# A softcap attention with a spectral mix on one core: the scores and values of the last 64 keys, and the fourth score burst, in other places of TensorE's order

## The chip, the cores and the metric

The kernel runs on one core of a Trainium2 chip. The metric is the device time of one execution in microseconds; the time given for a kernel is the median of its runs.

## The reference

For each of 8 batches and 12 heads, with 448 positions and a head size of 64, the attention is

```python
scores = cap * tanh((q @ k.T / 8) / cap)
attn = exp(scores - max) / sum
x = attn @ v
```

The heads are put side by side (x is 448 x 768 for a batch), and then comes a mix:

```python
theta = x @ w_theta
y = w_tok_r @ (x * cos(theta)) + w_tok_i @ (x * sin(theta))
u = x + y
out = u + relu(u @ w_ch)
```

Everything is float32.

## The kernel before

**Steps.** The attention is done in 24 steps, one for four heads (two pairs, i = 0 and 1; a pair is two heads h on the two halves of the partitions). Three steps make a batch. The mix of a batch runs four steps and more behind its attention, and its products fill TensorE while ScalarE makes tanh and exp: a step of the steady part carries either the theta products of a batch (T0 to T5), its token mixing (M0a to M5b) or its channel products (C0 to C5). What each engine does, and in which order, is written out by hand: `FRONT`, `PARTS` and `OTHER` (lines 539 to 563) are lists of words, one list for a step, and `pipeline` (565 to 655) issues the words one after the other. Each engine works through its own instructions in this order, and waits are only for data and for rooms. `PARTS[0]` is a theta step, `PARTS[1]` a mixing step, `PARTS[2]` a channel step; `OTHER` has the first steps (0, 3, 4, 5, 6) and the last two, 24 and 25, which have no attention. Step s finishes the values of step s - 1.

**Scores (S0 to S3, lines 262 to 291).** A head has 448 keys: three chunks of 128 and the last 64. `BURSTS` (228) says what each of the four bursts makes: S0 chunks 0 and 1 of pair 0, S1 chunk 2 of pair 0 and the last keys of both pairs, S2 chunks 0 and 1 of pair 1, S3 chunk 2 of pair 1. A chunk's matmul has 64 rows and 128 columns of the array, so that the two heads of a pair run side by side on its two halves; the last keys have 64 rows and 64 columns, so that four run side by side on its quarters. From step 7 on (`WHOLE`) the chunks are made from rounded halves of q and k (three products, one pass each); `prep_q` and `prep_k` (Pa, Pb) make these on VectorE. All bursts use one tile of four PSUM banks (pool `psS`, one buffer), so each waits until the tanh of the one before (t0 to t3, line 305) has read it out.

**Values (Vr, V0, W, lines 350 to 363).** The unnormalised output of pair i is an accumulator `a`, one bank of pool `psM`, which has four banks and from which every product, the sums `r` and the accumulators take theirs in turn. V0 and W are the 24 matmuls over the three chunks of pairs 0 and 1 (128 rows, 64 columns, two at once); Vr is the eight matmuls over the last keys of both pairs (64 rows, 64 columns, four at once), ahead of V0. cV0 and cV1 (365) copy the accumulators out on ScalarE, after which v of the next step is loaded. Ra and Rb (370) are the denominators' sums, I (392) inverts them on VectorE and spreads them by four DMAs on SP, N (411) multiplies. a0a to a1b (333) are VectorE's additions for the sums.

**The mix.** A theta product is 18 matmuls (128 rows and columns), y, d and sc make the angle and its cosine and sine, r (471) multiplies, f (475) transposes within blocks of 32, and D (`carry`, 485) carries the squares of 32 rows to their places: 16 DMAs of 56 KB for two of the six column blocks. D0 and D1 are at the end of a theta step, D2 is in the following mixing step, whose h and l words (495 to 511) make rounded halves of the carried data on ScalarE and VectorE for the products M. Three of four of these DMAs are issued on SP, one on GpSimd:

```python
queue = nc.gpsimd if (b < B - 1 or i) and d == 3 else nc.sync
```

Of the kernel before, what the change touches and what calls it, by code (L numbers as in the profile page):

```python
# [12 lines left out]
F32 = mybir.dt.float32  # L13
# [62 lines left out]
def softcap_attn_then_spectral_mix(ctx, tc, qk2, v, cap, w_theta, w_tok, w_ch, outT):  # L76
# [185 lines left out]
    def scores(s, n):  # L262
        t = spt[s, n] = psS.tile([P, 2, 2, 512], F32, tag="s", name=f"s{s}_{n}")
        for u, what in enumerate(BURSTS[n]):
            for i in (0, 1) if what is None else what[:1]:
                k = 2 * s + i
                out, cols = (t[i * D : (i + 1) * D, u], slice(REST, S)) if what is None else (t[:, u], slice(what[1] * P, (what[1] + 1) * P))
                if what is None and (k, "r") in Q:
                    products = ((Q.pop((k, "r")), raw[k, 0]),)
                elif what is None or s < WHOLE:  # L270
                    products = ((raw[k, 1][:, cols], raw[k, 0]),)
                else:
                    kk, qq = Q[k, "k"], Q[k, "q"]
                    products = [(kk[a][:, cols], qq[c]) for a, c in ((0, 0), (1, 0), (0, 1))]
                for m, (kk, qq) in enumerate(products):
                    for h in range(2):
                        rows = slice(h * D, (h + 1) * D)
                        nc.tensor.matmul(out[:, h, :S], kk[rows], qq[rows], start=m == 0, stop=m == len(products) - 1)  # L278
# [17 lines left out]
    def tanh(s, n):  # L296
# [8 lines left out]
        nc.scalar.activation(pp, spt.pop((s, n))[:, :m, :, :S], AF.Tanh, scale=qscale)  # L305
# [44 lines left out]
    def av_rest(s, pairs=(0, 1)):  # L350
        first = [av_room(s, i) for i in pairs][0]
        for i in pairs:
            rows = slice(i * D, (i + 1) * D)
            for h in range(2):
                nc.tensor.matmul(acc_of["a", s, i][h * D : (h + 1) * D, :S], vt[s][rows, 12 + h, :], U[s, None][rows, h, :],
                                 start=first or i == 1, stop=not first and i == 0)

# [127 lines left out]
    def carry(b, i):  # L485
# [46 lines left out]
    def chan_out(b, m):  # L532
# [19 lines left out]
        LEAD: "S0 t0 Y4 Y5 w2 cV0 e0 W Ra cV1 v Rb w0 Pa1 I S1 Pb1 q0 t1 e1 T0 y0 d0 a0a T1 y1 d1 S2 t2 w1 sc0 a0b T2 y2 r0 r1 f0 f1 D0 N d2"  # L552
        " T3 Pa0 S3 Pb0 q1 t3 y3 e2 e3 d3 a1a a1b sc1 T4 y4 d4 T5 y5 d5 w3 r2 r3 f2 f3 D1",
# [3 lines left out]
        LEAD + 2: "S0 t0 :#ch2a :ch2a :@ch3b Vr V0 u5 cV0 e0 :#ch2b :ch2b W Ra cV1 v :@ch4a :#ch3a :ch3a Rb :@ch4b Pa1 S1 Pb1 q0 t1 :#ch3b :ch3b C0 I c0 :@ch5a :*ch4a e1 C1 :*ch4b :@ch5b"  # L557
        " S2 t2 :ch4a c1 C2 :*ch5a :*ch5b :ch4b e2 :ch5a C3 S3 c2 t3 :ch5b Pa0 Pb0 q1 N- c3 C4 e3 N c4 X0 X1 X2 X3 C5 X4 X5 c5",
# [6 lines left out]
    def pipeline(general):  # L565
# [5 lines left out]
        def run(s, b, word):  # L571
# [21 lines left out]
            elif word in ("Vr", "V0", "W"):  # L593
                if done:
                    if word == "W" and ("a", k, 1) not in acc_of:
                        av_rest(k, (1,))
                        used(k, "Vr")
                    if word == "Vr":
                        av_rest(k)
# [115 lines left out]
```

## Time and profile before

| | |
|---|---|
| median of 3 runs | 909.82 us (907.93 to 910.62) |
| the profiled execution's own time | 907.38 us |
| its span, first to last instruction | 905.5 us |
| granted TensorE clock, mean over the span | 0.999 of full speed |
| matmul instructions | 4896 |

In the rows below, PE is TensorE, DVE is VectorE, ACT is ScalarE, POOL is GpSimd and SP is SyncE, whose queue issues most of the DMAs; a q behind a name (SPq) is the engine's sequencer. L278 is line 278 of the kernel: the scores; L355 and L362 are the values, L389 the sums, L431 to L433 the theta and channel products, L519 to L521 the mixing products, L492 the squares' DMAs, L407 the DMAs of the inverted sums. The ends of matmuls are modelled and overlap the next one's start; the starts are what to compare.

### The profile page before, as it was taken

The page shows a single profiled execution, that of the slowest core. Times are in us where ns is not written, and L with a number is a line of the kernel's source. Part 1 is how long each engine was busy: PE and PEld are TensorE (multiplying, and loading weights), DVE is VectorE, ACT ScalarE, POOL GpSimd, SP SyncE. Part 2 cuts the span into 40 slices and gives each one's busy share as a digit, 9 for nine tenths or more (in the row PEclk, how much of TensorE's full clock was granted, in tenths as well). Part 3 has the DMA queues.
Part 4 walks back from the last instruction along what each step waited for, and adds up shares of the span by engine and source line. Part 5 has one row for each costly group of instructions (what it writes and reads, how often), then busy time and mean ns, then how long its engine had stood idle before and what let it go on. Part 6 is the DMA issues. An engine that isn't in the chain of part 4 may idle for free.

```text
span 905.5 us, 13212 instructions
## 1 busy us (share of the span) xinstructions
PE 892.0 (99%) x4896; PEld 638.5 (71%) x4896; DVE 657.3 (73%) x1095; ACT 572.3 (63%) x633; POOL 53.1 (6%) x109
## 2 busy tenths in 40 slices
PE   8999999999999999999999999999999999999997
PEld 4235575757758668677686686776876867779996
DVE  6899859969866598675985678855986659765741
ACT  6887865569845597547965488545894459733420
POOL 0000111100100011000100000000010000100100
PEclk9999999999999999999999999999999999999999
DMA  7653373442423325222442233333242331410411
GB/s 267 203 187 86 101 176 108 149 130 55 123 71 93 92 56 158 63 82 72 105 120 66 79 89 114 82 92 92 71 120 55 112 92 52 110 44 25 111 40 64
DMA packets 51947, 90.70 MB, mean 100 GB/s; under 512 B 10913, under 2 KB 44833, under 8 KB 51873
## 3 DMA queue, kind: packets, MB, share of 16 engines
q1 hardware_dynamic: 44592, 69.21, 26.8%
q0 software_dynamic: 3824, 9.61, 4.0%
q10 hardware_dynamic: 3456, 10.95, 3.9%
q8 instruction: 40, 0.66, 0.3%
q14 instruction: 35, 0.28, 0.1%
HBM read 45.68 MB, written 11.01 MB: 63 GB/s over the span
## 4 chain that ended last, share of the span: by engine, by line
PE 72%; DVE 16%; SPq 3%; issue 3%; DMA 3%; ACT 3%; DVEq 0%; ACTq 0%
PE s L278 11%; PE a L362 10%; PE ch L431 7%; PE ch L433 6%; PE ch L432 6%; PE mx L521 5%; PE th L431 5%; PE mx L519 4%; PE th L432 4%; PE mx L520 4%; PE th L433 4%; PE r L389 3%; SPq L492 3%; DVE g_row L481 2%; DMA t<-g_row 2%
## 5 line engine op out<-in xcount | busy, mean ns | idle before, releaser
L305 ACT ACTIVATE p<-s,qscale 128x1792 f32<-128x1792 f32 (+1 forms) x77 | 117.0, 1520 | 102.9 <-PE s L278 93.3
L519 PE MATMUL mx<-wtk_h,zh 128*128 128x448 f32 x336 | 125.1, 372 | 3.9 <-ACT zh L502 3.9
L521 PE MATMUL mx<-wtk_h,zl 128*128 128x448 f32 x336 | 123.9, 369 | 1.0 <-DVE zl L509 0.6
L520 PE MATMUL mx<-wtk_l,zh 128*128 128x448 f32 x336 | 123.0, 366 | 0.0
L318 ACT ACTIVATE p<-p,cap_sb 128x1792 f32<-128x1792 f32 (+1 forms) x77 | 119.9, 1559 | 2.6 <-PE a L362 1.9
L431 PE MATMUL th<-xs,wth_h 128*128 128x448 f32 x288 | 107.5, 373 | 0.0
L431 PE MATMUL ch<-us,wch_h 128*128 128x448 f32 x288 | 107.4, 373 | 0.0
L432 PE MATMUL th<-xs,wth_h 128*128 128x448 f32 x288 | 105.5, 366 | 0.0
L433 PE MATMUL ch<-us,wch_l 128*128 128x448 f32 x288 | 105.5, 366 | 0.0
L432 PE MATMUL ch<-us,wch_h 128*128 128x448 f32 x288 | 105.3, 366 | 0.0
L433 PE MATMUL th<-xs,wth_l 128*128 128x448 f32 x288 | 105.3, 365 | 0.0
L362 PE MATMUL a<-p,v 128*64 128x448 f32 x496 | 102.6, 545 | 0.0
L362 PEld LDWEIGHTS a<-p,v 128*64 128x64 f32 x496 | 33.1, 136 | 63.9 <-issue 62.5
L519 PEld LDWEIGHTS mx<-wtk_h,zh 128*128 128x128 f32 x336 | 63.1, 188 | 19.1 <-ACT zh L502 7.4
L492 POOL DMA_DIRECT2D t<-g_row x76 | 38.5, 513 | 588.8 <-DVE x_row L414 156.7
L502 ACT CAST zh<-t 128x512 fp32r<-128x512 f32 x84 | 44.6, 560 | 41.6 <-DMA t<-g_row 12.4
L521 PEld LDWEIGHTS mx<-wtk_h,zl 128*128 128x128 f32 x336 | 63.1, 188 | 9.6 <-DVE zl L509 4.4
L520 PEld LDWEIGHTS mx<-wtk_l,zh 128*128 128x128 f32 x336 | 63.1, 188 | 5.1
L431 PEld LDWEIGHTS th<-xs,wth_h 128*128 128x128 f32 x288 | 54.1, 188 | 14.2 <-issue 5.1
L431 PEld LDWEIGHTS ch<-us,wch_h 128*128 128x128 f32 x288 | 54.1, 188 | 13.6 <-issue 2.9
L509 DVE TENSOR_TENSOR zl<-t,zh 128x512 fp32r<-128x512 f32 x84 | 50.1, 616 | 16.7 <-ACT zh L502 9.4
L535 DVE SCALAR_TENSOR_TENSOR x<-ch,x 128x448 f32<-128x448 f32 x43 | 26.7, 622 | 48.3 <-PE ch L433 48.3
(517 smaller groups left out, 1563.5 us busy)
## 6 DMA issues: line engine op xcount, KB each, us to landing
t<-g_row SPq DMA_DIRECT2D x228, 56.0 KB, 2.0
k<-in_qk SPq DMA_DIRECT2D x47, 224.0 KB, 3.4
v<-in_v ACTq DMA_DIRECT2D x23, 448.0 KB, 3.3
out_dram<-x SPq DMA_DIRECT2D x43, 224.0 KB, 1.9
q<-in_qk SPq DMA_DIRECT2D x42, 224.0 KB, 2.8
bc<-ri SPq DMA_DIRECT2D x68, 112.0 KB, 2.3
t<-g_row POOLq DMA_DIRECT2D x76, 56.0 KB, 2.1
x_row<-ri SPq DMA_DIRECT2D x24, 112.0 KB, 2.3
```

The lines of the kernel that those rows point to most:

```text
L278: nc.tensor.matmul(out[:, h, :S], kk[rows], qq[rows], start=m == 0, stop=m == len(products) - 1)
L305: nc.scalar.activation(pp, spt.pop((s, n))[:, :m, :, :S], AF.Tanh, scale=qscale)
L318: nc.scalar.activation(pp, pp, AF.Exp, scale=cap_sb)
L362: nc.tensor.matmul(acc_of["a", s, i][h * D : (h + 1) * D, :S], vt[s][:, 6 * i + 3 * h + c, :], U[s, (i, c)][:, h, :], start=first and c == ...
L431: nc.tensor.matmul(acc[:, :S], wh[:, j, ms], t[:, 0, :], start=j == 0, stop=False)
L432: nc.tensor.matmul(acc[:, :S], wh[:, j, ms], t[:, 1, :], start=False, stop=False)
L433: nc.tensor.matmul(acc[:, :S], wl[:, j, ms], t[:, 0, :], start=False, stop=j == NJ - 1)
L492: queue.dma_start(t[32 * m : 32 * m + 32, d * S : (d + 1) * S], f[32 * d : 32 * d + 32, m * S : (m + 1) * S])
L509: nc.vector.tensor_tensor(zl, tokens(b, j)[:, c0:c1], zh.bitcast(F32), op=ALU.subtract)
L519: nc.tensor.matmul(acc[:, :S], zh, wtk_h[:, c, :], start=c == 0, stop=False)
L520: nc.tensor.matmul(acc[:, :S], zh, wtk_l[:, c, :], start=False, stop=False)
L521: nc.tensor.matmul(acc[:, :S], zl, wtk_h[:, c, :], start=False, stop=c == NC2 - 1)
```

## The change

The score bursts: in steps 4 and 6 to 23 the fourth burst S3 is written to two banks of the accumulators' pool `psM` and not to the tile of four banks; in the order it stands right behind S2, and its tanh (two instructions, one a bank) behind S2's. Inside S1 the last keys come first. The values: in steps 6 to 23 Vr comes last, behind the sums, as the closing matmuls of both accumulators (`av_last`), right ahead of S1; cV0 and cV1 move behind it. The squares: for all batches but the first, GpSimd issues two of four (d = 2 and 3) instead of one. In the mixing step some words change places with these: I moves ahead of f4, t1 behind h1b, a0a and a0b behind l3b and l4b.

```diff
--- before.py
+++ after.py
@@ -260,11 +260,15 @@
                 load_raw(k + 1, 1)
 
     def scores(s, n):
-        t = spt[s, n] = psS.tile([P, 2, 2, 512], F32, tag="s", name=f"s{s}_{n}")
-        for u, what in enumerate(BURSTS[n]):
+        if n == 3 and (s == LEAD or s > LEAD + 1):
+            t = spt[s, n] = [psM.tile([P, 512], F32, tag="m", name=f"s{s}_{n}{h}") for h in range(2)]
+        else:
+            t = spt[s, n] = psS.tile([P, 2, 2, 512], F32, tag="s", name=f"s{s}_{n}")
+        for u, what in sorted(enumerate(BURSTS[n]), key=lambda at: at[1] is not None):
             for i in (0, 1) if what is None else what[:1]:
                 k = 2 * s + i
-                out, cols = (t[i * D : (i + 1) * D, u], slice(REST, S)) if what is None else (t[:, u], slice(what[1] * P, (what[1] + 1) * P))
+                rows, cols = (slice(i * D, (i + 1) * D), slice(REST, S)) if what is None else (slice(0, P), slice(what[1] * P, (what[1] + 1) * P))
+                out = [t[h][rows] if isinstance(t, list) else t[rows, u, h] for h in range(2)]
                 if what is None and (k, "r") in Q:
                     products = ((Q.pop((k, "r")), raw[k, 0]),)
                 elif what is None or s < WHOLE:
@@ -275,7 +279,7 @@
                 for m, (kk, qq) in enumerate(products):
                     for h in range(2):
                         rows = slice(h * D, (h + 1) * D)
-                        nc.tensor.matmul(out[:, h, :S], kk[rows], qq[rows], start=m == 0, stop=m == len(products) - 1)
+                        nc.tensor.matmul(out[h][:, :S], kk[rows], qq[rows], start=m == 0, stop=m == len(products) - 1)
         k = 2 * s + n // 2
         if n % 2 and s < WHOLE:
             for part in range(2):
@@ -302,7 +306,11 @@
             pp = wk.tile([P, 1, 2, S], F32, tag="p1", name=f"p{s}_{n}", bufs=1)
         for u, what in enumerate(BURSTS[n]):
             U[s, what] = pp[:, u]
-        nc.scalar.activation(pp, spt.pop((s, n))[:, :m, :, :S], AF.Tanh, scale=qscale)
+        t = spt.pop((s, n))
+        for h, each in enumerate(t if isinstance(t, list) else ()):
+            nc.scalar.activation(pp[:, 0, h], each[:, :S], AF.Tanh, scale=qscale)
+        if not isinstance(t, list):
+            nc.scalar.activation(pp, t[:, :m, :, :S], AF.Tanh, scale=qscale)
         U[s, "t", n] = pp
 
     def used(s, word):
@@ -354,6 +362,12 @@
             for h in range(2):
                 nc.tensor.matmul(acc_of["a", s, i][h * D : (h + 1) * D, :S], vt[s][rows, 12 + h, :], U[s, None][rows, h, :],
                                  start=first or i == 1, stop=not first and i == 0)
+
+    def av_last(s):
+        for i in range(2):
+            rows = slice(i * D, (i + 1) * D)
+            for h in range(2):
+                nc.tensor.matmul(acc_of["a", s, i][h * D : (h + 1) * D, :S], vt[s][rows, 12 + h, :], U[s, None][rows, h, :], start=False, stop=True)
 
     def av(s, i):
         first = av_room(s, i)
@@ -488,7 +502,7 @@
         f, t = Z[b, i, "f"], Z[b, i, "t"]
         for m in range(4):
             for d in range(4):
-                queue = nc.gpsimd if (b < B - 1 or i) and d == 3 else nc.sync
+                queue = nc.gpsimd if (b < B - 1 or i) and d >= (2 if b else 3) else nc.sync
                 queue.dma_start(t[32 * m : 32 * m + 32, d * S : (d + 1) * S], f[32 * d : 32 * d + 32, m * S : (m + 1) * S])
         large.give(Z.pop((b, i, "f")))
 
@@ -538,24 +552,24 @@
 
     FRONT = "S0 t0 q0 q1 W cV0 v w0 e0 S1 t1 Ra cV1 e1 w1 S2 t2 Rb I Vr^ e2 S3 t3 V0^ w2 e3 w3 N"
     PARTS = (
-        "S0 t0 Vr V0 cV0 e0 W Ra cV1 v Rb w0 Pa1 I S1 Pb1 q0 t1 w1 e1 T0 y0 d0 a0a T1 y1 d1 sc0 S2 t2 a0b T2 y2 r0 r1 f0 f1 D0 N d2"
-        " e2 T3 y3 Pa0 S3 Pb0 q1 t3 e3 d3 a1a a1b sc1 T4 y4 d4 T5 y5 d5 r2 r3 f2 f3 D1",
-        "S0 t0 Vr V0 h0a l0a h0b l0b W h1a Ra Rb cV0 cV1 v sc2 Pa1 S1 Pb1 q0 t1 M0a l1a r4 h1b M0b r5 l1b f4 f5 D2 e0 h2a M1a l2a e1 M1b h2b l2b m0 I w1"
-        " S2 t2 M2a h3a l3a m1 a0a M2b h3b l3b u0 e2 u1 a0b M3a h4a l4a M3b h4b l4b Pa0 m2 w2 S3 q1 t3 M4a Pb0 h5a l5a u2 m3 M4b"
+        "S0 t0 V0 e0 W Ra Rb Vr cV0 cV1 v w0 Pa1 I S1 Pb1 q0 t1 w1 e1 T0 y0 d0 a0a T1 y1 d1 sc0 S2 S3 t2 t3 a0b T2 y2 r0 r1 f0 f1 D0 N d2"
+        " e2 T3 y3 Pa0 Pb0 q1 e3 d3 a1a a1b sc1 T4 y4 d4 T5 y5 d5 r2 r3 f2 f3 D1",
+        "S0 t0 V0 h0a l0a h0b l0b W h1a Ra Rb Vr cV0 cV1 v sc2 Pa1 S1 Pb1 q0 M0a l1a r4 h1b t1 M0b r5 l1b I f4 f5 D2 e0 h2a M1a l2a e1 M1b m0 h2b l2b w1"
+        " S2 S3 t2 M2a h3a l3a t3 m1 M2b h3b l3b a0a u0 e2 u1 M3a h4a l4a M3b h4b l4b a0b m2 Pa0 w2 q1 M4a Pb0 h5a l5a u2 m3 M4b"
         " h5b l5b u3 e3 a1a M5a m4 u4 M5b a1b w3 m5",
-        "S0 t0 Vr V0 u5 cV0 e0 W Ra cV1 v Rb w0 Pa1 S1 Pb1 q0 t1 N- C0 c0 e1 a0a w1 C1 c1 I S2 t2 a0b C2 c2 w2 N e2 C3 Pa0 c3 S3 Pb0 q1 t3 X0 X1 a1a"
+        "S0 t0 V0 u5 e0 W Ra Rb Vr cV0 cV1 v w0 Pa1 S1 Pb1 q0 t1 N- C0 c0 e1 a0a w1 C1 c1 I S2 S3 t2 t3 a0b C2 c2 w2 N e2 C3 Pa0 c3 Pb0 q1 X0 X1 a1a"
         " C4 c4 e3 X2 X3 w3 a1b X4 C5 X5 c5",
     )
     OTHER = {
         0: "v S0 t0 q0 q1 w0 e0 S1 t1 e1 w1 S2 t2 Vr^ e2 S3 t3 V0^ w2 e3 w3",
         LEAD - 1: "S0 t0 q0 q1 W cV0 v w0 e0 S1 t1 Ra cV1 e1 w1 S2 t2 Rb I Vr^ e2 S3 t3 V0^ e3 X0 X1 X2 X3 N w2 w3",
-        LEAD: "S0 t0 Y4 Y5 w2 cV0 e0 W Ra cV1 v Rb w0 Pa1 I S1 Pb1 q0 t1 e1 T0 y0 d0 a0a T1 y1 d1 S2 t2 w1 sc0 a0b T2 y2 r0 r1 f0 f1 D0 N d2"
-        " T3 Pa0 S3 Pb0 q1 t3 y3 e2 e3 d3 a1a a1b sc1 T4 y4 d4 T5 y5 d5 w3 r2 r3 f2 f3 D1",
+        LEAD: "S0 t0 Y4 Y5 w2 cV0 e0 W Ra cV1 v Rb w0 Pa1 I S1 Pb1 q0 t1 e1 T0 y0 d0 a0a T1 y1 d1 S2 S3 t2 w1 t3 sc0 a0b T2 y2 r0 r1 f0 f1 D0 N d2"
+        " T3 Pa0 Pb0 q1 y3 e2 e3 d3 a1a a1b sc1 T4 y4 d4 T5 y5 d5 w3 r2 r3 f2 f3 D1",
         LEAD + 1: "S0 t0 Vr V0 Ra h0a l0a h0b l0b W h1a Rb :%ch0a cV0 cV1 :@ch0b sc2 Pa1 S1 Pb1 q0 t1 v M0a l1a r4 h1b M0b r5 l1b f4 f5 D2 e0 h2a M1a l2a m0 :#ch0a :0ch0a e1 M1b h2b l2b :1ch0a"
         " S2 t2 M2a h3a :2ch0a :@ch1a l3a M2b h3b l3b I m1 M3a h4a l4a :#ch0b :0ch0b M3b h4b l4b :1ch0b e2 m2 S3 q1 t3 M4a h5a l5a :2ch0b :@ch1b :#ch1a :0ch1a m3 M4b"
         " h5b l5b u0 u1 e3 :1ch1a M5a :2ch1a :@ch2a m4 u2 M5b :@ch2b :#ch1b :0ch1b m5 u3 :1ch1b :2ch1b u4 :@ch3a",
-        LEAD + 2: "S0 t0 :#ch2a :ch2a :@ch3b Vr V0 u5 cV0 e0 :#ch2b :ch2b W Ra cV1 v :@ch4a :#ch3a :ch3a Rb :@ch4b Pa1 S1 Pb1 q0 t1 :#ch3b :ch3b C0 I c0 :@ch5a :*ch4a e1 C1 :*ch4b :@ch5b"
-        " S2 t2 :ch4a c1 C2 :*ch5a :*ch5b :ch4b e2 :ch5a C3 S3 c2 t3 :ch5b Pa0 Pb0 q1 N- c3 C4 e3 N c4 X0 X1 X2 X3 C5 X4 X5 c5",
+        LEAD + 2: "S0 t0 :#ch2a :ch2a :@ch3b V0 u5 e0 :#ch2b :ch2b W Ra Rb Vr cV0 cV1 v :@ch4a :#ch3a :ch3a :@ch4b Pa1 S1 Pb1 q0 t1 :#ch3b :ch3b C0 I c0 :@ch5a :*ch4a e1 C1 :*ch4b :@ch5b"
+        " S2 S3 t2 t3 c1 :ch4a C2 :*ch5a :*ch5b :ch4b e2 :ch5a C3 c2 :ch5b Pa0 Pb0 q1 N- c3 C4 e3 N c4 X0 X1 X2 X3 C5 X4 X5 c5",
         NS: "Vr V0 u5 N- W cV0 cV1 Ra Rb I C0 c0 X0 X1 C1 c1 X2 X3 C2 c2 N X4 X5 T0+ y0+ d0+ T1+ y1+ d1+ sc0+ T2+ r0+ r1+ f0+ f1+ D0+ y2+ d2+ T3+"
             " y3+ d3+ sc1+ T4+ r2+ r3+ f2+ f3+ y4+ d4+ T5+ D1+ y5+ d5+ h0a+ l0a+ h0b+ l0b+ sc2+ C3 c3 r4+ r5+ f4+ f5+ D2+ C4 h1a+ l1a+ c4 C5 c5",
         NS + 1: "M0a h1b M0b l1b h2a m0 u0 M1a l2a h2b M1b l2b h3a m1 u1 M2a l3a h3b M2b l3b h4a m2 u2 M3a l4a h4b M3b l4b h5a"
@@ -592,11 +606,11 @@
                     used(s, word[:2])
             elif word in ("Vr", "V0", "W"):
                 if done:
-                    if word == "W" and ("a", k, 1) not in acc_of:
+                    if word == "W" and ("a", k, 1) not in acc_of and k < LEAD:
                         av_rest(k, (1,))
                         used(k, "Vr")
                     if word == "Vr":
-                        av_rest(k)
+                        av_last(k) if ("a", k, 0) in acc_of else av_rest(k)
                     else:
                         av(k, 0 if word == "V0" else 1)
                     used(k, word)
```

## Rows read from the trace of the kernel before

**Rows 1.** The page's busy time, share of the span, instructions.
```profile
PE 892.0 (99%) x4896; PEld 638.5 (71%) x4896; DVE 657.3 (73%) x1095; ACT 572.3 (63%) x633; POOL 53.1 (6%) x109
```

**Rows 2.** The page's chain that ended last, by engine.
```profile
PE 72%; DVE 16%; SPq 3%; issue 3%; DMA 3%; ACT 3%; DVEq 0%; ACTq 0%
```

**Rows 3.** TensorE's waits: us in total, times, longest us.
```profile
PE mx L519 <- ACT zh L502: 3.9, 5, 1.3
```

**Rows 4.** TensorE's timeline, S2 of a theta step: start us, us.
```profile
313.58 0.47 PE L278 MATMUL s<-q21h,k21h 64*128 64x448 f32 x2
...
315.00 0.47 PE L431 MATMUL th<-xs,wth_h 128*128 128x448 f32 x1
315.31 0.37 PE L432 MATMUL th<-xs,wth_h 128*128 128x448 f32 x1
315.51 0.37 PE L433 MATMUL th<-xs,wth_l 128*128 128x448 f32 x1
```

**Rows 5.** The same timeline, S3 of that step.
```profile
322.54 0.48 PE L278 MATMUL s<-q21h,k21h 64*128 64x448 f32 x2
...
323.36 0.47 PE L431 MATMUL th<-xs,wth_h 128*128 128x448 f32 x1
```

**Rows 6.** The same timeline, the values and the last keys' scores.
```profile
297.88 0.98 PE L355 MATMUL a<-g_row,v 64*64 64x448 f32 x8
298.79 1.72 PE L362 MATMUL a<-p,v 128*64 128x448 f32 x8
300.34 0.92 PE L362 MATMUL a<-g_row,v 128*64 128x448 f32 x4
301.10 2.42 PE L362 MATMUL a<-p,v 128*64 128x448 f32 x12
...
305.15 0.59 PE L278 MATMUL s<-q,r 64*64 64x448 f32 x2
...
306.06 0.47 PE L431 MATMUL th<-xs,wth_h 128*128 128x448 f32 x1
```

**Rows 7.** ScalarE's timeline in another theta step: T0's read-out, t2.
```profile
417.01 0.55 ACT L455 ACTIVATE z<-th 128x448 f32<-128x448 f32 x1 [0.25 <-PE th L433]
...
426.58 1.76 ACT L305 ACTIVATE p<-s,qscale 128x1792 f32<-128x1792 f32 x1
```

**Rows 8.** SP's timeline in a mixing step: D1, D2, the inverted sums.
```profile
661.68 7.49 SPq L492 DMA_DIRECT2D t<-g_row  x12
...
673.49 7.53 SPq L492 DMA_DIRECT2D t<-g_row  x12
681.13 3.29 SPq L407 DMA_DIRECT2D bc<-ri  x4
```

**Rows 9.** GpSimd's timeline there: its part of D2.
```profile
674.00 1.96 POOL L492 DMA_DIRECT2D t<-g_row  x4 [9.81 <-DVE zl L509]
```

**Rows 10.** VectorE's timeline there: f4 and f5, and the wait before.
```profile
671.25 2.11 DVE L481 STREAM_TRANSPOSE g_row<-z 128x896 f32<-128x896 f32 x2 [2.44 <-DMA t<-g_row]
```

**Rows 11.** Groups of instructions, the inversion's second transpose: busy us, mean ns.
```profile
L403 DVE STREAM_TRANSPOSE ri<-few 128x448 f32<-128x448 f32 x23 | 14.8, 645 | 0.8
```

**Rows 12.** The page's DMA issues: count, KB, median us to landing.
```profile
t<-g_row SPq DMA_DIRECT2D x228, 56.0 KB, 2.0
...
t<-g_row POOLq DMA_DIRECT2D x76, 56.0 KB, 2.1
```

**Rows 13.** ScalarE's timeline in that mixing step: h4a, h4b and the wait before.
```profile
683.95 1.03 ACT L502 CAST zh<-t 128x512 fp32r<-128x512 f32 x2 [4.85 <-DMA bc<-ri]
```

**Rows 14.** TensorE's timeline there: S3 and the start of M4.
```profile
682.46 0.47 PE L278 MATMUL s<-q41h,k41h 64*128 64x448 f32 x2
...
684.62 0.47 PE L519 MATMUL mx<-wtk_h,zh 128*128 128x448 f32 x1 [1.29 <-ACT zh L502]
684.93 0.37 PE L520 MATMUL mx<-wtk_l,zh 128*128 128x448 f32 x1
685.35 0.47 PE L521 MATMUL mx<-wtk_h,zl 128*128 128x448 f32 x1
```

## The prediction

> **What bounds the kernel now.** I read the page's busy shares first: TensorE is busy for 99% of the span [rows 1], and the chain that ended last runs through it for 72% [rows 2]. So a microsecond counts only where TensorE's own sequence gets shorter or where it waits. The list of its waits is short: the largest entry, the token mixing waiting for ScalarE's rounded halves, is 3.9 us in five places [rows 3]. There are thus two places for a gain: what TensorE spends between blocks of different shape, which counts as busy, and that one wait.
>
> The first is seen in starts, not in busy time, because the ends of matmuls are modelled. Burst S2 (six pairs of 64x128 matmuls, two half-arrays at once) takes 313.58 to 315.00, 1.42 us [rows 4]; S3 (three pairs) takes 322.54 to 323.36, 0.82 us [rows 5]. The difference, 0.60 for three pairs, is 0.20 a pair, so each block carries 0.22 us beside its pairs. The products around it pay too: the first matmul after the burst is followed at 0.31 us, the second at 0.20 [rows 4], and the 36 between the bursts take 315.00 to 322.54 [rows 4, 5], 7.54 us, where 36 at 0.204 (the 0.20 of the rows, averaged inside the products) would be 7.34. A burst that stands alone between products therefore costs 0.22 + 0.20 = 0.42 us above its pairs.
>
> The same for the last keys. Their eight value matmuls (64x64, four quarters at once) take 297.88 to 298.79, 0.91 us; their eight score matmuls 305.15 to 306.06, again 0.91 [rows 6]. One round is 0.38 us by the value matmuls, of which four (two rounds) take 300.34 to 301.10 [rows 6]. Two rounds are 0.76, which leaves 0.15 for getting in and out of the shape.
>
> **The change, part by part.**
> S3 behind S2: steps 4 and 6 to 23 put S3 right behind S2, in the same shape, so 19 times one entry and exit goes: 19 x 0.42 = 8.0 us. I take 0.41 (7.8), since S3's pairs start in banks of another pool.
> Values and scores of the last keys side by side: steps 6 to 23 move Vr behind Rb, and S1 now begins with its 64x64 part. The number of blocks drops by one: 16 matmuls in one shape are 4 x 0.38 + 0.15 = 1.67 instead of 1.82. 18 x 0.15 = 2.7 us. Inside S1 the two shapes change places, which is neutral, in the front steps too.
> What follows from the moved Vr: both accumulators close later, so cV0 and cV1 come after e0 on ScalarE and the sines of the mixing step start about 1.4 us later against the products. That delays r4, not TensorE: the matmuls of M0 and M1 cover it. The load of v is issued behind cV1, about 1.5 us later; a whole step (over 20 us) hides it.
> t3 split in two: a 448-column read-out of one bank takes 0.55 us [rows 7], so 1.1 for the pair, a tenth more than before, on an engine that isn't the bound. Cover: in a theta step t2 starts at 426.58 and takes 1.76 [rows 7], so both halves are out by about 429.4, the first by 428.9. T4, which by rotation takes that first bank, begins about 430.1: T0 ended as ScalarE read it at 417.0, T1 takes 3.7 us, S2 and S3 2.0, T2 and T3 7.4. If that cover goes, T4 waits.
> S3's second bank was the sums' bank r. In channel steps the inversion that reads it stands behind c1 on VectorE, just as S2 ends; bounds 0 to 0.15 us, seven times. I take nothing.
> The squares (D): of 16 transfers SP now issues 8 and GpSimd 8, in all batches but the first. SP needed 7.49 us for the 12 of D1 and 7.53 for those of D2 [rows 8], 0.63 each; eight are 5.0. GpSimd needs 1.96 for four [rows 9]; eight are 3.9. D1 is therefore through 2.5 us earlier, and f4, which waited 2.44 us for it [rows 10], is freed. The inversion now stands ahead of f4 on VectorE: two transposes of 0.645 us [rows 11] and a small reciprocal, about 1.6. VectorE is free at 668.8 (f4's 671.25 less its wait), so f5 ends near 672.5, not 673.4. On SP the inversion's four broadcasts (3.29 us today, behind D2 [rows 8]) now run ahead, from 670.4 to 673.7; then eight squares to 678.7 instead of 681.0. They land about two microseconds later [rows 12], near 680.7.
> Who waits for D2: the rounded half h4a started at 683.95 [rows 13], and the mixing product M4 at 684.62, with S3's first pair at 682.46, instead of 0.82 us behind it; it loses 1.34 us, and another 0.32 at once (684.93 to 685.35 is 0.42 where 0.20 is usual, and 0.31 instead of 0.20 before it) [rows 14]. With the change M4 is due near 682.9 (684.62 less 1.34 and 0.42) and D2 is there 2 us before that. Of the 3.9 us I leave 0.3 to step 5, whose transfers stay as they are; 3.6 go, and four times 0.3 behind them: 4.8.
> What is late next: M5. Its second halves come off VectorE behind the inversion, two sums for the denominators and the next pair's q and k; my count leaves them no slack. I charge 1.0 us over six mixing steps; below that nothing, above it today's whole wait, 3.9.
> Sum: 7.8 + 2.7 + 4.8 - 1.0 = 14.3 us. The profiled execution's own time is 907.38 (span 905.5 and 1.9 around it), so it would be 893.1; the median of the runs is 2.4 higher, and 909.82 - 14.3 = 895.5.
>
> **The rivals.**
> *The waits stay* (0.24). Mixing steps hang on a chain of ScalarE and VectorE that the change makes tighter: t1 comes behind h1b, t3 ahead of h3b and h4a. If it binds as D2 did, only the shapes pay: 7.8 + 2.7 = 10.5, 899.3. For it: the count for M5. Against: ScalarE stood idle for 4.85 us before h4a [rows 13].
> *The GpSimd half comes late* (0.07). Then M4 waits for the other queue: today's 3.9 stays and up to 1.3 more in each of six steps, 10.5 - 7.8 = 2.7, 907. The median time to landing speaks against it: 2.1 us from GpSimd, 2.0 from SP [rows 12].
> The Trainium skill, "SBUF — State Buffer", section "SBUF: two separate sides", says that a VectorE instruction in a two-port mode locks GpSimd out of the port it writes descriptors through, so that such transfers wait for VectorE; by that rule this rival would be likely, since the casts of q and k run beside D1. The trace doesn't show it at the median; no run here shows eight in a row.
> *The shapes give half* (0.08). Banks of another pool could make the switch inside S2 and S3, or inside the 64x64 block, cost something. 3.9 + 1.4 + 3.8 = 9.1, 900.7. Against it: in today's S2 the pairs already go from one bank to the next at an unbroken 0.20.
> *The banks run out* (0.05), the slower case. S3 takes two of the four banks that the accumulators turn over in. If the product behind S3 got one of them it would wait for t2 and both halves of t3, 1.76 + 1.1 less some cover, about 2.6 us, 19 times: 49 - 14, near 945. The point from which it decides is a wait of 0.75 us a step (14.3 / 19): up to there the gain is only eaten. Against it: ScalarE reads T0's bank only at 417.01, released by T0's last matmul [rows 7], while T1 must already be running; the list of waits from which rows 3 is taken names no theta product, so the bank given out is not the one freed last.
> *More than forecast* (0.06): the waits of step 5 and 6 go as well and M5 is in time, 17 us, 893.
>
> **How the numbers follow.** The forecast (895.5) has 0.50; its own range, from the unknown of M5 and of the waits, is 893 to 898. With the first and third rival the range goes to about 901.5, and to 903 for a GpSimd queue that costs part of its price; below, the larger gain and a median that scatters by 1 to 2 us give 890.5. What is left out is about 0.13. A measurement of this kernel can tell about 0.3% (2.7 us) from no change. Faster by more than that: forecast, first, third and last case and part of the second, 0.91; the rest of the second 0.04; the banks 0.05.
>
> **What would show it.** Right: S2 and S3 as one block of nine pairs in about 2.03 us, products after it unbroken to the next S0; one block of 16 64x64 matmuls in 1.67; SP's D2 in 5 us; no wait of mixing for ScalarE over 0.3. Wrong: a first matmul of a product waiting for a read-out by ScalarE (banks), a gap before M4 or M5 (chain), GpSimd's transfers landing well behind SP's, or nine pairs in over 2.2 us.

## The result, and the profile after

The changed kernel runs in 899.62 us (median of 6 runs, 899.1 to 899.97); the kernel before in 907.88 (6 runs, 906.68 to 910.62: the three of before and three more). The ratio is 0.9903, interval 0.989 to 0.9917: 1.0% faster. The profiled execution took 899.28 us, its span is 897.4, 8.1 less than before.

First the page's busy time of the changed kernel and its chain by engine, which answer to [rows 1, 2]:

```profile
PE 881.5 (98%) x4896; PEld 644.0 (72%) x4896; DVE 659.2 (73%) x1095; ACT 573.5 (64%) x652; POOL 91.5 (10%) x189
...
PE 85%; DVE 6%; DMA 3%; SPq 2%; ACT 1%; issue 1%; ACTq 0%; DVEq 0%
```

TensorE is busy 10.5 us less and idle more. The list of its waits after (total, times, longest) answers to [rows 3]. The line numbers have shifted: scores L282, sums L403, values of the last keys L370, theta and channel products L445 to L447, squares' DMAs L506, ScalarE's rounded halves zh L516, VectorE's zl L523, mixing products L533 to L535, their read-out L541, channel read-out L549.

```profile
PE mx L535 <- DVE zl L523: 2.1, 4, 0.7
PE mx L533 <- DVE x_row L541: 1.8, 2, 1.3
PE fill L124 <- DVE qscale L101: 1.0, 1, 1.0
PE fill L124 <- POOL ones_sb L127: 0.9, 1, 0.9
PE s L282 <- ACT g_row L313: 0.9, 1, 0.9
PE mx L533 <- DVE x L541: 0.8, 2, 0.5
PE ch L445 <- DVE x L549: 0.5, 1, 0.5
```

The entry of 3.9 us is gone. In its place stand two kinds of wait that both end on VectorE: mixing products for their second halves (zl), and mixing products for a read-out of an earlier one (x_row and x of L541), that is for a bank. Both kinds are in mixing steps. One of the four waits for zl, 0.66 in step 5, is an old one, which the list of before has as:

```profile
PE mx L521 <- DVE zl L509: 0.6, 1, 0.6
```

Next TensorE's timeline of the changed kernel, first the last keys, then S2 with S3 behind it in the same theta step as [rows 4 to 6] (start us, us):

```profile
301.83 0.98 PE L370 MATMUL a<-g_row,v 64*64 64x448 f32 x8
302.64 0.54 PE L282 MATMUL s<-q,r 64*64 64x448 f32 x1
...
303.50 0.47 PE L282 MATMUL s<-q20h,k20h 64*128 64x448 f32 x2
...
311.84 0.47 PE L282 MATMUL s<-q21h,k21h 64*128 64x448 f32 x2
...
313.57 0.37 PE L282 MATMUL s<-q21l,k21h 64*128 64x448 f32 x2
313.86 0.47 PE L445 MATMUL th<-xs,wth_h 128*128 128x448 f32 x1
```

The sixteen 64x64 matmuls take 301.83 to 303.50, 1.67 us; nine pairs take 311.84 to 313.86, 2.02 us. Both are the lengths that were predicted, and the products behind run unbroken.

Where the 8.1 us of the span came from is seen when both traces are cut at the same place. I cut at the start of each step's sums (r), so that "step 8" runs from its sums to those of step 9; "squares alone" is experiment 2 below and "best" experiment 11.

| stretch, us | before | squares alone | after | best |
|---|---|---|---|---|
| start to the first sums | 27.69 | 28.18 | 28.91 | 27.98 |
| steps 1 to 3 | 44.60 | 44.61 | 44.61 | 44.60 |
| step 4 | 35.55 | 35.55 | 35.19 | 35.16 |
| step 5 | 45.51 | 44.38 | 43.95 | 43.76 |
| step 6 | 39.01 | 39.09 | 39.10 | 39.02 |
| 11 theta and channel steps, 7 to 22 | 381.25 | 381.29 | 375.17 | 375.17 |
| 6 mixing steps (8, 11, ... 23) | 233.42 | 227.28 | 229.92 | 225.09 |
| last sums to last matmul | 92.69 | 92.69 | 92.70 | 92.68 |
| last matmul to the end | 5.78 | 6.14 | 7.85 | 8.14 |

The cut shifts one block between two rows. The eight value matmuls of the last keys, 0.91 us as a block of their own [rows 6], stand ahead of the sums of step 6 before and behind them in the changed kernel; in step 24 both kernels have them ahead. So in the columns "after" and "best" step 5 is 0.9 too short, and the mixing steps (the last of them, step 23) are 0.9 too long.

A theta or channel step became 0.55 us shorter ((381.25 - 375.17) / 11). The mixing steps became 3.5 shorter together by the table and 4.4 with the shift put right; a kernel with only the squares gains 6.1 there, and the shapes, at 0.55 a step, should add 3.3. The start is 1.2 longer and the end 2.1.

A mixing step shows what took the gain. In step 14 of the changed kernel, TensorE:

```profile
452.80 0.47 PE L282 MATMUL s<-q29h,k29h 64*128 64x448 f32 x2
...
454.52 0.36 PE L282 MATMUL s<-q29l,k29h 64*128 64x448 f32 x2
456.20 0.44 PE L533 MATMUL mx<-wtk_h,zh 128*128 128x448 f32 x1 [1.32 <-DVE x_row L541]
```

and VectorE in the same stretch:

```profile
448.79 0.55 DVE L523 TENSOR_TENSOR zl<-t,zh 128x384 fp32r<-128x384 f32 x1
449.26 0.64 DVE L409 STREAM_TRANSPOSE ri<-r 128x448 f32<-128x448 f32 x1
...
452.84 2.11 DVE L495 STREAM_TRANSPOSE g_row<-z 128x896 f32<-128x896 f32 x2 [1.99 <-DMA q<-in_qk]
454.87 0.65 DVE L523 TENSOR_TENSOR zl<-t,zh 128x512 fp32r<-128x512 f32 x1
455.44 0.61 DVE L541 TENSOR_TENSOR x_row<-mx,x_row 128x448 f32<-128x448 f32 x1
```

M2 is due 0.29 us after S3's last pair and comes 1.38 later than that: it wants the bank of M0, whose products had ended long before, but whose read-out m0 (455.44) stands in VectorE's order behind f4 and f5 (452.84) and l2a. f4 still waits 1.99 us for its room in the squares' source (2.83 in this step before; in the step of [rows 10] 0.65 is left of 2.44). The releaser that the row names is only the last by the profile: the transfers of D1 must be out of that tile, and the last of them lands at 452.42. D1 is on ScalarE's, SP's and GpSimd's queues of that step:

```profile
442.64 0.33 ACTq L236 DMA_DIRECT2D v<-in_v  x1
```
```profile
442.76 6.75 SPq L506 DMA_DIRECT2D t<-g_row  x8
...
455.08 4.98 SPq L506 DMA_DIRECT2D t<-g_row  x8
```
```profile
443.25 3.96 POOL L506 DMA_DIRECT2D t<-g_row  x8 [11.82 <-ACT x L381]
```

The eight of D2 go out in 4.98 us as predicted (7.53 for twelve in [rows 8]), the eight of D1 in 6.75 here and in about 5.0 in four of the six steps. The load of v (448 KB) now starts 0.12 us ahead of D1; before it led by 0.63 in this step. From the first issue to the last landing D1 takes 8.3 to 9.7 us over the six mixing steps, before 8.8 to 9.5: on average it got 0.4 shorter, not 2.5. The page's landing times after, for [rows 12]:

```profile
t<-g_row SPq DMA_DIRECT2D x152, 56.0 KB, 2.6
t<-g_row POOLq DMA_DIRECT2D x152, 56.0 KB, 2.3
```

Both queues are slower at the median (2.0 and 2.1 before), and GpSimd's is the faster one.

### The profile page after: what moved, and what is told of

Same layout as the page of the kernel before. It is cut to its first block, busy times and chain, and to the rows that moved or that the text cites. A ratio compares the mean times of both kernels' runs of the same rounds, so it can differ in the third digit from the quotient of the medians.

```text
span 897.4 us, 13316 instructions
## 1 busy us (share of the span) xinstructions
PE 881.5 (98%) x4896; PEld 644.0 (72%) x4896; DVE 659.2 (73%) x1095; ACT 573.5 (64%) x652; POOL 91.5 (10%) x189
## 4 chain that ended last, share of the span: by engine, by line
PE 85%; DVE 6%; DMA 3%; SPq 2%; ACT 1%; issue 1%; ACTq 0%; DVEq 0%
PE s L282 13%; PE a L376 12%; PE th L445 7%; PE th L446 7%; PE ch L445 7%; PE th L447 7%; PE ch L447 6%; PE ch L446 6%; PE mx L533 5%; PE mx L535 5%; PE mx L534 5%; PE r L403 4%; PE a L370 2%; SPq L506 2%; DMA t<-g_row 1%
## 5 line engine op out<-in xcount | busy, mean ns | idle before, releaser
L313 ACT ACTIVATE p<-s,qscale 128x1792 f32<-128x1792 f32 (+1 forms) x58 | 98.0, 1690 | 96.6 <-PE s L282 87.1
L506 POOL DMA_DIRECT2D t<-g_row x152 | 74.8, 499 | 542.0 <-DVE x_row L428 224.3
L533 PE MATMUL mx<-wtk_h,zh 128*128 128x448 f32 x336 | 124.3, 370 | 2.7 <-DVE x_row L541 1.8
L535 PE MATMUL mx<-wtk_h,zl 128*128 128x448 f32 x336 | 123.4, 367 | 2.1 <-DVE zl L523 2.1
L445 PE MATMUL ch<-us,wch_h 128*128 128x448 f32 x288 | 106.8, 371 | 0.5 <-DVE x L549 0.5
L445 PE MATMUL th<-xs,wth_h 128*128 128x448 f32 x288 | 106.8, 371 | 0.0
L447 PE MATMUL ch<-us,wch_l 128*128 128x448 f32 x288 | 105.4, 366 | 0.0
L447 PE MATMUL th<-xs,wth_l 128*128 128x448 f32 x288 | 105.4, 366 | 0.0
L533 PEld LDWEIGHTS mx<-wtk_h,zh 128*128 128x128 f32 x336 | 63.1, 188 | 13.6 <-ACT zh L516 5.4
L535 PEld LDWEIGHTS mx<-wtk_h,zl 128*128 128x128 f32 x336 | 63.1, 188 | 9.0 <-DVE zl L523 3.6
L549 DVE SCALAR_TENSOR_TENSOR x<-ch,x 128x448 f32<-128x448 f32 x43 | 26.6, 621 | 48.7 <-PE ch L447 48.7
L523 DVE TENSOR_TENSOR zl<-t,zh 128x512 fp32r<-128x512 f32 x84 | 50.4, 617 | 15.4 <-ACT zh L516 11.9
L445 PEld LDWEIGHTS ch<-us,wch_h 128*128 128x128 f32 x288 | 54.1, 188 | 10.0 <-issue 3.8
L445 PEld LDWEIGHTS th<-xs,wth_h 128*128 128x128 f32 x288 | 54.1, 188 | 9.4 <-issue 3.7
L475 DVE SCALAR_TENSOR_TENSOR z<-z 128x448 f32<-128x448 f32 x48 | 29.8, 621 | 41.0 <-ACT z L470 40.8
```

The source lines that it names most:

```text
L313: nc.scalar.activation(pp, t[:, :m, :, :S], AF.Tanh, scale=qscale)
L445: nc.tensor.matmul(acc[:, :S], wh[:, j, ms], t[:, 0, :], start=j == 0, stop=False)
L447: nc.tensor.matmul(acc[:, :S], wl[:, j, ms], t[:, 0, :], start=False, stop=j == NJ - 1)
L506: queue.dma_start(t[32 * m : 32 * m + 32, d * S : (d + 1) * S], f[32 * d : 32 * d + 32, m * S : (m + 1) * S])
L523: nc.vector.tensor_tensor(zl, tokens(b, j)[:, c0:c1], zh.bitcast(F32), op=ALU.subtract)
L533: nc.tensor.matmul(acc[:, :S], zh, wtk_h[:, c, :], start=c == 0, stop=False)
```

## The experiments

Each ratio is to runs of the kernel before beside the experiment. The experiments ran on four chips, so small differences of their medians are read together with the traces.

**1. The shapes without the squares.** The changed kernel with the squares' queues of before; the new orders stay.

```diff
-d >= (2 if b else 3)
+d == 3
```

> The changed kernel, with three of four squares' DMAs on SP again. Theory A (D1 lands late because v's 448 KB are loaded beside it, not because SP issues slowly): D1 lands about 9 us after its first issue as it does with the half on GpSimd (8.3 to 9.7), so M2's waits for its bank (3.0 us in six mixing steps) stay; D2 is issued in 7.5 us instead of 5.0 behind the four broadcasts and M4 and M5 wait up to 1 us more in some steps: 900 to 903, the blocks of 18 and 16 as they are. Theory B (the half on GpSimd is what the forecast's 3.8 us hang on): M4 waits in all six steps as before the change, 903 to 905. Theory C (GpSimd's descriptors are the late part): D1 lands earlier than now and the kernel gets faster, 897 to 899.

Measured: 915.93 us (915.66 to 916.6), ratio 1.0092, interval 1.0075 to 1.0109: slower than before, and slower than any of the three theories had it. TensorE's waits of it, and its timeline in step 14:

```profile
PE mx L533 <- ACT zh L516: 6.3, 4, 2.2
...
PE mx L533 <- DVE x_row L541: 4.1, 3, 2.4
PE mx L535 <- DVE zl L523: 4.1, 5, 1.1
PE mx L533 <- DVE x L541: 2.5, 3, 1.5
```
```profile
463.91 0.45 PE L533 MATMUL mx<-wtk_h,zh 128*128 128x448 f32 x1 [2.44 <-DVE x_row L541]
...
464.61 0.57 PE L533 MATMUL mx<-wtk_h,zh 128*128 128x448 f32 x1
464.97 0.58 PE L534 MATMUL mx<-wtk_l,zh 128*128 128x448 f32 x1
```

Theta and channel steps are as short as after (33.87), so the shapes' gain is there; the mixing steps take 248.7 us, 14 more than before (0.9 of the difference is the cut). M4 waits for ScalarE again, and M2 for its bank more than twice as long as in the changed kernel; D1 lands 8.8 to 10.6 us after its first issue. Part of it is the clock: behind the wait of 2.44 us nine matmuls start 0.37 us apart instead of 0.20, and the granted clock from 464.7 to 467.9 is 0.50, the lower of its two levels (1.2 GHz of 2.4). The same follows in step 17 behind a wait of 2.20.

**2. The squares alone.** The kernel before, with only this line changed.

```diff
-d == 3
+d >= (2 if b else 3)
```

> The kernel before, with nothing but half of the squares on GpSimd. All shapes stay, so PE's blocks are those of before (S3 alone 0.82, the 64x64 blocks 0.91 each). Theory A: D1 lands as late as before (8.8 to 9.5 us after its first issue) and f4 starts as late; D2 is issued 2.5 us faster and M4's waits, 6.1 us in six steps with what follows them, mostly go: 4 to 6 us faster, 902 to 904. Theory C: the half on GpSimd lands late, M4 waits as before, no change, 906 to 909.

Measured: 901.3 us (900.98 to 901.92), ratio 0.9931 (0.9915 to 0.9948), 6.8 us less. Of mixing one wait is left:

```profile
PE mx L521 <- DVE zl L509: 0.2, 1, 0.2
```

That one is in step 5. So GpSimd's eight in a row cost nothing that TensorE sees, and the wait of [rows 3] was SP's queue. All waits on VectorE from step 8 on in the changed kernel come from the rest of the change. Theory A missed one thing: D1 lands 7.1 to 8.1 us after its first issue here, not 8.8 to 9.5. With v 0.6 to 0.7 us ahead, as before, eight issues on SP do get D1 through earlier.

**3. The read-out of M0 ahead of f4.** The changed kernel, mixing step:

```diff
-I f4 f5 D2 e0 h2a M1a l2a e1 M1b m0 h2b l2b
+I m0 f4 f5 D2 e0 h2a M1a l2a e1 M1b h2b l2b
```

> The changed kernel, with m0 (VectorE's sum that reads out M0's bank) ahead of f4 in the mixing step instead of behind f4, f5 and l2a. Theory A: M2 waits for M0's bank only because m0 stands behind f4, which waits for D1; with m0 ahead M2 starts 0.29 us after S3's last pair, at most one step still waits 0.5 us for l2a: 2 to 3 us faster, 896.5 to 897.5. Rival: M2 hangs on D1 itself by way of l2a; then the wait moves from the first to the third matmul of M2 and 0 to 1 us is gained, 898.5 to 899.6.

Measured: 897.85 us (895.89 to 898.71), ratio 0.9889 (0.9869 to 0.991). That is 1.8 us under the changed kernel by the medians; the intervals overlap, and the traces decide: the mixing steps take 228.3 us, 1.6 less. The waits for L541 are gone from the list, and only this one of mixing is left:

```profile
PE mx L535 <- DVE zl L523: 2.8, 4, 1.1
```

In step 14 the read-out starts at 449.30, right behind the inversion, and M2 0.29 us after S3's last pair: the bank's wait was the order on VectorE. Part of the 3.0 us comes back at M5, whose third matmul is now 0.58, 0.84 and 1.28 late in three steps (0.78, 0.57 and 0.57 in the changed kernel).

**4. The load of v later.** The changed kernel, mixing step, v away from D1:

```diff
-Ra Rb Vr cV0 cV1 v sc2
+Ra Rb Vr cV0 cV1 sc2
...
-e2 u1 M3a
+e2 u1 v M3a
```

> The changed kernel, with v's load in the mixing step issued behind u1 instead of behind cV1, where it met D1. Theory A (contention with v's 448 KB): D1 lands 6.5 to 7 us after its first issue instead of 8.3 to 9.7, f4 starts about 2 us earlier, m0 with it, M2 waits for no bank and l5a is earlier: 3 to 4.5 us faster, 895 to 896.5. Theory C (VectorE keeps GpSimd from its descriptors, or the queues are slow by themselves): D1 lands as late as now, 899 to 900. If v is late for the next step's values instead, V0 waits and it is slower.

Measured: 902.49 us (902.32 to 902.65), ratio 0.9943 (0.9926 to 0.9959): slower than the change, which neither theory A nor C had. TensorE's waits of mixing in it:

```profile
PE mx L535 <- DVE zl L523: 6.0, 6, 1.1
...
PE mx L533 <- ACT zh L516: 0.4, 1, 0.4
```

SP's timeline, step 17, and under it GpSimd's part of D1 and the first cast there:

```profile
550.08 4.95 SPq L506 DMA_DIRECT2D t<-g_row  x8
...
560.94 5.69 SPq L506 DMA_DIRECT2D t<-g_row  x8
```
```profile
550.60 3.94 POOL L506 DMA_DIRECT2D t<-g_row  x8 [12.10 <-PE s L282]
```
```profile
551.13 0.39 DVE L241 CAST q35h<-q 128x448 fp32r<-128x448 f32 x1
```

Both halves of the theory on v are in it. Away from v, D1 has landed 6.5 to 7.3 us after its first issue (8.3 to 9.7 in the changed kernel), and the waits for L541 are gone although m0 still stands behind f4. Where v now falls, D2 lands 8.0 to 9.3 us after its first issue instead of 6.5 to 7.7, and the second halves of M5 come 1.2 to 1.3 late in five of the six steps (the sixth entry is step 5). The casts of q and k stay beside D1, and GpSimd issues its eight among them in 3.94 us, so they are not what held it.

**5. l5a ahead of the next pair's q and k.** The changed kernel, mixing step:

```diff
-Pa0 w2 q1 M4a Pb0 h5a l5a u2
+w2 q1 M4a h5a l5a Pa0 Pb0 u2
```

> The changed kernel, with VectorE's half l5a ahead of the next pair's q and k (Pa0, Pb0, 2.1 us) instead of behind them. Theory A: M5's waits (2.2 us in three steps, its third matmul, the first that needs l5a) hang on this order alone and go; M2's waits stay 3.0 us: 897 to 897.8. Rival: h5a on ScalarE or the data set l5a, then M5 waits as now, 899 to 900.

In step 17 of the changed kernel, M5's third matmul, and VectorE from the casts of the next q and k to l5a:

```profile
575.57 0.47 PE L535 MATMUL mx<-wtk_h,zl 128*128 128x448 f32 x1 [0.41 <-DVE zl L523]
```
```profile
572.92 0.37 DVE L241 CAST q36h<-x_row 128x448 fp32r<-128x448 f32 x1
...
574.84 0.68 DVE L523 TENSOR_TENSOR zl<-t,zh 128x512 fp32r<-128x512 f32 x1
```

Measured: 897.41 us (896.95 to 898.1), ratio 0.9884 (0.9867 to 0.99). M5's waits for zl go (the one left is step 5's), M2's for the bank stay:

```profile
PE mx L533 <- DVE x_row L541: 2.4, 3, 1.5
...
PE mx L533 <- DVE x L541: 0.9, 2, 0.5
...
PE mx L535 <- DVE zl L523: 0.4, 1, 0.4
```

**6. Both orders mended** (the edits of 3 and 5 together).

> Both orders on VectorE together: m0 ahead of f4, l5a ahead of Pa0 and Pb0. Theory A: all of the mixing waits that the change brought are queue order on VectorE; 5.3 us less one wait for l2a of 0.4: 894.5 to 895.5. Rival: with the first waits gone TensorE comes to M4 earlier than D2's data, and M4 waits instead, 896 to 898.

Measured: 894.81 us (893.58 to 895.09), ratio 0.9858 (0.9841 to 0.9874). No mixing step from 8 on has an entry in the list of waits: they take 37.5 to 37.8 us and the last 37.05, where the changed kernel has up to 38.9. The one entry of mixing, 0.6, is in step 5.

**7. And v behind h5a.** Experiment 6 with v moved between D1 and the next step, behind D2's landing.

```diff
-cV0 cV1 v sc2
+cV0 cV1 sc2
...
-M4a h5a l5a Pa0
+M4a h5a v l5a Pa0
```

> As the run before, and v's load behind h5a, clear of D1 and of D2. If v's load is what makes D1 land 8.3 to 9.7 us after its first issue and D2 up to 9 when it was moved there, both land within 7 us of their first issue and no mixing product waits at all: 893.5 to 895. If the load is too late for the next step's V0, V0 waits once a batch: 896 or more.

Measured: 893.9 us (893.85 to 893.95), ratio 0.9846 (0.983 to 0.9863). The mixing steps take 224.9 us, as in experiment 6 (225.0), and 0.9 us under its median is within its scatter: once nothing urgent hangs on D1, v's place hardly counts.

**8. S3 at its old places.** The changed kernel with S3 in the score tile and at its old places in all steps; the squares, the moved Vr and the mixing order stay.

```diff
-if n == 3 and (s == LEAD or s > LEAD + 1):
+if False:
...
-sc0 S2 S3 t2 t3 a0b T2
+sc0 S2 t2 a0b T2
...
-T3 y3 Pa0 Pb0 q1 e3
+T3 y3 Pa0 S3 Pb0 q1 t3 e3
```

> The changed kernel with the fourth burst back in the tile of four banks and at its old place, so only Vr, the squares and the order of the mixing step are new. Theory A (M2 needs m0 early only because S3 takes two of the accumulators' four banks): no mixing product waits; the kernel with the squares alone (901.3) less 2.7 to 3.0 for the blocks of sixteen: 898.3 to 899. Rival (the new order or the later Vr brings the waits): 900 to 903, with waits of M2 for m0 as in the changed kernel.

Measured: 901.37 us (899.35 to 902.58), ratio 0.9933 (0.9917 to 0.995). The median misses what was expected and the runs scatter over 3 us, so it says nothing on a term of 2.7; the trace does, though it is of the fastest of four (899.35) and the other three were not traced. Theta and channel steps take 34.26 us here, 34.43 in experiment 2 and 33.87 after: the 64x64 block is worth 0.17 a step, S3's move 0.39. And no product waits for L541; it is S3's two banks that make M2 need M0's.

**9. Steps 5 and 6 too.** Experiment 7, with the first splits of batch 0's channel weights moved: in step 5 behind l5b, in step 6 behind t1.

```diff
-:2ch0b :@ch1b :#ch1a :0ch1a m3 M4b h5b l5b u0
+:2ch0b :@ch1b m3 M4b h5b l5b :#ch1a :0ch1a u0
...
-:@ch4a :#ch3a :ch3a :@ch4b Pa1 S1 Pb1 q0 t1
+:@ch4a Pa1 S1 Pb1 q0 t1 :#ch3a :ch3a :@ch4b
```

> The run with m0, l5a and v moved (893.9), and two orders in the steps that the change had left: in step 5 l5b ahead of the weights' splits that follow M4a, in step 6 the split of ch3a behind t1. If these queue orders are what makes M5 wait 0.8 us in step 5 and S2 0.9 in step 6, 1 to 1.8 us are gained: 892 to 893. If the splits themselves (their work, not their place) are the bound there, 0: 893.5 to 894.5.

Measured: 893.7 us (893.56 to 895.79), ratio 0.9841 (0.9824 to 0.9858): no gain over experiment 7. Step 5 is 0.95 shorter (43.0) and step 6 0.8 longer (39.9), with one new wait:

```profile
PE s L282 <- DVE ri L409: 1.2, 1, 1.2
```

S3 there waits for the sums' bank, whose inversion now comes later: what one order gives, the next takes back.

**10. The mended orders without the squares.** Experiment 6 with `d == 3`.

> The run with m0 and l5a moved (894.8), with three of four squares' DMAs on SP again. Theory A: the queue order and SP's issuing are separate causes; with the order mended D2's twelve issues behind the four broadcasts (3.3 + 7.5 us) still bring h4a 2 us and more behind TensorE in each of six steps: 901 to 906, the wait at M4 and none at M2. Rival: the 915.9 of the changed kernel with these DMAs on SP was the order's doing, 895 to 898.

Measured: 912.85 us (911.69 to 914.8), ratio 1.0054 (1.0034 to 1.0074), worse than expected. The bank's wait is gone, and M4 is late in every mixing step:

```profile
PE mx L533 <- ACT zh L516: 8.9, 6, 2.1
PE mx L535 <- DVE zl L523: 2.8, 5, 1.2
```

The six mixing steps take 245.0 us, 20 more than with the squares (experiment 6: 225.0). The two waits are 11.4 of it (0.3 of the second is step 5's). Some 4 us more are half pace: in three steps (11, 17 and 20) seven to nine matmuls behind the wait start 0.37 us apart, 0.17 too many each, at a granted clock of 0.50. The rest is not split.

**11. The old order of shapes in the front.** Experiment 7, with the last keys first in S1 only from step 4 on.

```diff
-key=lambda at: at[1] is not None)
+key=lambda at: at[1] is not None and s >= LEAD)
```

> The best version so far (read-out of M0 ahead of f4, l5a ahead of the proj splits, load of v behind h5a: 893.9), with the order of the two shapes inside S1 as in the kernel before in steps 0 to 3. Why: the prediction called the new order neutral in the front steps, but the S1 of step 0 takes 2.79 us by TensorE's starts (11.24 to 14.03) where it took 1.86 (10.92 to 12.78), since the last keys' scores of the second matrix are now asked for before its load is there. Theory (order against a load): S1 of step 0 back to about 1.9 us, the first sums at about 27.7 to 28.2 us instead of 28.64, time lower by 0.5 to 0.9, about 893.2. Rival (the front's loads scatter by themselves): the first sums stay at 28.4 to 29.1, time 893.9 within 0.5.

Measured: 893.62 us (893.2 to 893.82), ratio 0.9836 (0.9819 to 0.9853). TensorE's timeline, first S1, before the edit (experiment 7):

```profile
9.14 0.97 PE L282 MATMUL s<-x_row 64*64 64x448 f32 x4 [0.18 <-ACT p L313]
11.89 0.97 PE L282 MATMUL s<-q,k 64*64 64x448 f32 x4 [1.78 <-DMA k<-in_qk]
```

and with it:

```profile
11.20 1.55 PE L282 MATMUL s<-x_row 64*128 64x448 f32 x6
...
13.07 1.75 PE L124 MATMUL fill<-ones_sb 128*32 128x112 f32 x16
```

S1 is back at 1.87 us (11.20 to 13.07) and the first sums start at 27.98 instead of 28.64, as the order theory has it. The time moves by 0.3, which alone would not show it. This is the lowest median of all versions, not clear of experiments 7 and 9.

**12. GpSimd's program twelve transfers shorter.** Experiment 7, with batch 1 as before.

```diff
-d >= (2 if b else 3)
+d >= (2 if b > 1 else 3)
```

> The same best version with the squares of batch 1 back at three quarters on SP, so that GpSimd's program is shorter by some 12 transfers. Why: from the start of the last matmul to the end of the span the kernel before takes 5.8 us, the squares alone 6.1, the shapes alone 5.8, and every kernel that has both 7.7 to 7.9, with one or two fetches of code more in that stretch. Theory (the length of a program decides at the end): that stretch falls back to about 6, which gives 1.8 us; the M4 of the first mixing step waits again for up to 1.6 us and the one after it not, so about 893.7 in all, the stretch itself being the test. Rival (the end is longer for another reason than GpSimd's length): the stretch stays at 7.7 to 7.9 and the time is 894 to 895.5.

Measured: 894.3 us (893.91 to 896.27), ratio 0.9856 (0.9837 to 0.9875). The wait of M4 is back in the first mixing step, which is 2.4 longer (39.99):

```profile
PE mx L533 <- ACT zh L516: 1.4, 1, 1.4
```

The last matmul starts at 886.25 in a span of 892.0: 5.75 us to the end, where experiment 7 has 7.89. The stretch answered as the theory on the program's length has it; the time is the rival's.

## Why the prediction was right, and where its sum was not

The direction held, and the time lies in the range; the sum of 14.3 us was too large, and the forecast's own 893 to 898 was missed. The span lost 8.1, the medians differ by 8.3. (899.62 is 10.2 under the 909.82 that the forecast started from; three more runs put the median of the kernel before 1.9 lower.) The four signs for right came: nine pairs in 2.02, sixteen 64x64 in 1.67, SP's D2 in 4.98 in the step shown, no wait of mixing for ScalarE. Of the signs for wrong one came as well: a gap before M5's third matmul. That the time lies within 0.4 us of a rival's 899.3 is luck: the losses at the start and the end, 3.3 us together, were in no case of the forecast.

**The shapes, 7.8 + 2.7: right.** 0.41 + 0.15 = 0.56 a step was claimed; 0.55 was found, split 0.39 and 0.17 by experiment 8. The fall of TensorE's busy time, 10.5, is no further proof: the slower matmuls right behind a wait (0.31 and 0.42 us in [rows 14]) count as busy too. The rival in which the shapes give half is out.

**The squares, 4.8: right in kind, too small alone.** By themselves they gave 6.8 (experiment 2), 6.1 of it in the mixing steps. Of the 1.3 over the forecast there, 0.8 is step 23, whose waits of under 0.1 us are not in [rows 3]. M4 no longer waits for ScalarE in the changed kernel, and D2 leaves SP in 4.98 us. The rival of a late GpSimd is out: its transfers land at 2.3, SP's at 2.6. By the rule of the Trainium skill, "SBUF — State Buffer", section "SBUF: two separate sides", they should have waited behind VectorE's casts. The traces don't bear that out here: what did slow D1 went away with v's load while the casts stayed (experiment 4).

**"What is late next", 1.0 charged: the step that failed.** Mixing steps should have given 7.2 (6 x 0.56 from the shapes, 4.8, less 1.0) and gave 4.4: 3.3 from the shapes, 6.1 from the squares, less some 5 for the waits that took the place. The 5 is 229.92 in the changed kernel against 225.0 with two orders mended. Three statements of that part were wrong or missing.
- "D1 is therefore through 2.5 us earlier, and f4 ... is freed". The issue on SP got shorter; the landing got 0.4 shorter, because the same change pushed the load of v onto D1 (with v where it was, experiment 2 has 1.5 less). "A whole step hides it" looked at who waits for v and not at what v lands beside. Experiment 4 shows it from both sides.
- M2's bank was not in the sum. S3 takes two of the four banks, so M2 needs M0's, and m0 stood behind f4. The starts of M2 are late by 0.53, 0.53, 1.38, 0.17, 0.05 and 0.39 us in the six steps, 3.0. The rival of banks running out asked only about tanh in theta steps; in mixing steps it came true through VectorE's order, 3.0 us in six steps, where 14.3 in nineteen would have turned the sign. Experiments 3 and 8 show it.
- M5: "my count leaves them no slack" was right, the size was not. Its third matmul is late by 0.78, 0.57 and 0.57 in three of the six steps, with what follows them some 2.2 us. Experiment 5 shows that it is l5a behind the casts of q and k.

**"Neutral, in the front steps too": wrong by about 0.7.** The last keys of the second matrix are asked for before they are loaded (experiment 11: the first sums at 28.64 and 27.98). The start of the changed kernel is 1.2 longer; up to 0.5 of that is scatter, since it appears with the squares alone.

**The end, not in the sum: 2.1.** From the last matmul to the end the span takes 5.8 to 6.3 us in the kernel before, the shapes alone, the squares alone and experiment 8, and 7.7 to 8.1 in all others that have both parts in full. Experiment 12 brings it back. Which program's length decides is open.

**Step 5** gave 0.65 us with the shift of the cut put right, where I left it alone, and 1.1 with the squares alone; the queues of its squares are the same in all versions. In the trace of before its D2 lands 12.2 us after the first issue, in the thirteen others 10.7 to 11.5, and only there M4 waits in that step (0.29). So this looks like scatter of one execution and not like the change. Step 6 gave nothing where I counted 0.56: there C2 waits 0.45 for a channel read-out (L549) and S2 0.2 longer for ScalarE. Together: 14.3 + 0.65 (step 5) - 0.65 (step 6) - 2.8 (mixing) - 1.2 (start) - 2.1 (end) - 0.1 = 8.1.

The halves of the change are not a sum of parts either. Shapes alone are 0.9% slower than before, squares alone 0.7% faster, both 1.0%, both with the two orders mended 1.4%. The rival in which the waits stay named the nearest time, 899.3, and not the cause: what bound was not ScalarE's chain behind t1 and t3 but VectorE's order and one load.

The split tanh, t3's banks and the sums' bank in channel steps were costed at nothing, and no wait in the steps from 7 on speaks against it.

## What to carry to other kernels

When a product moves into a rotation of buffers, recount who takes the buffer next: a read-out that had a whole rotation of slack becomes urgent, and must go up in its engine's order, above anything there that waits for a DMA. When a step is moved, look at what its transfers will land beside, not only at who waits for them. The cost of a change of matmul shape can be read from the starts around a block, and held to 0.05 us in every step here where nothing waits behind it.

## What the runs showed of the hardware

- A load of 448 KB issued with sixteen transfers of 56 KB slows them on both queues. GpSimd's eight of D1 land 4.0 to 5.8 us after their issue (medians of the six steps) beside it, and 2.1 to 3.3 with the load moved away (experiment 4); all sixteen are through in 8.3 to 9.7 and 6.5 to 7.3 us.
- Waits of TensorE of 1.46 to 2.44 us were followed by seven to nine matmuls at half pace, at a granted clock of 0.50, in steps 14 and 17 of experiment 1 and in three steps of experiment 10. Behind others of 1.55 to 1.70 us in the same two experiments, and behind the 1.41 of experiment 12 (granted clock 1.00 in both windows from 250 to 258), the pace stayed at 0.20. A late step can thus cost more than its wait.
- The end of the span was two us shorter with twelve GpSimd transfers less (experiment 12). In the last 9 us one queue fetches five blocks of code in every version with the long end and four in every version with the short one. GpSimd's length alone does not decide: it is the full one in experiments 2 and 8, where the end is short. The cause stays open.
